# Recutting the inverse-transform stage of a two-layer spectral/MLP kernel: one tile at a time, work moved between three engines, and the DMA loads of the MLP weights moved

## The chip, the cores and the metric

The kernel runs on one core of one Trainium2 chip. The metric is the device time of one execution in microseconds (us). Engine names are those of the profile: PE is TensorE's matrix multiply, PEld its weight load, DVE is VectorE, ACT is ScalarE, POOL is GpSimd, SP is SyncE, which here only issues DMAs. A line number such as L462 is a line of the kernel that the profile belongs to, so the same statement has other numbers in other kernels.

Most executions of a kernel agree within about 0.3%, but one of the first four of the kernel before took 1096.59 us, in a state with a granted TensorE clock of 0.655 of full speed. That state is called slow. It happens to be the one that the profile caught.

## The reference, cut to what matters

```python
def _A_ref(x, w_r, w_i):                      # spectral mixer, x is (1, 2048, 576)
    X = rfft2(x.astype(float32), axes=(-2, -1))
    X = X * (w_r + 1j * w_i)
    return irfft2(X, s=(2048, 576)).astype(bfloat16)

def _B_ref(x, w1, b1, w2, b2):                # MLP, 576 -> 4608 -> 576
    y = layernorm(x)
    return gelu(y @ w1 + b1) @ w2 + b2

x = x + _A_ref(layernorm(x)); x = x + _B_ref(layernorm(x))      # layer 0
x = x + _A_ref(layernorm(x)); x = x + _B_ref(layernorm(x))      # layer 1
```

The transforms are done as matrix products. The 2048 rows are 16 tiles of 128 rows. The stage of interest is the end of `_A_ref`, once per layer: for each tile a short inverse transform along the rows (the "first product"), then the inverse transform along the 576 columns (the "second product"), which gives an even and an odd half of 288 columns. The result is x[:288] += even + odd and x[288:] += even - odd. The first four tiles are then normalised and transposed for the MLP, whose first matmul is the end of the stage.

## The kernel before

Two pools share PSUM: three big tiles of 4 KiB a partition (`big_ps`) and two small ones of half that size (`sm_ps`).

```python
def idft_v(n):                      # first product, two tiles at once
    quad, half = QUADS[n // 2], n % 2
    pu = big_ps([P, 2, 2, 2, 128])
    # ... 8 matmuls of 256 columns
    u2 = work.tile([P, 2, 2, 2, 128], BF16, tag="turn")
    nc.scalar.copy(out=u2[:], in_=pu[:])

def idft_v_rest(q):                 # last frequencies of four tiles
    # ... 16 matmuls of 128 columns into two groups of 34 partitions
    for p0 in (0, 64):
        nc.scalar.copy(out=u2r[p0 : p0 + 34], in_=pr[p0 : p0 + 34])

def idft_k(n):                      # second product and the sums, two tiles
    for i2 in range(2):
        po = big_ps([P, 2, 512])
        # ... 6 matmuls of 288 columns
        nc.vector.tensor_tensor(out=tt[:], in0=po[:, 0:1, 0:DH].to_broadcast([P, 2, DH]), in1=xr, op=ALU.add)
        marks["out", t] = nc.vector.tensor_tensor(out=xr[:, 0], in0=tt[:, 0], in1=po[:, 1, 0:DH], op=ALU.add).ins
        nc.vector.tensor_tensor(out=xr[:, 1], in0=tt[:, 1], in1=po[:, 1, 0:DH], op=ALU.subtract)

keep_busy(14)                       # matmuls on zeros while the last exchange lands
for n in range(9):
    if n < 8:
        idft_v(n)
        if n % 2 == 0: idft_v_rest(n // 2)
    if n >= 1: idft_k(n - 1)
    if n == 2: prep.stats_act()         # 8 passes on ScalarE: sum and square sum of 4 tiles
    if n == 3: prep.scale_act()
    if 4 <= n < 8: prep.norm_act(n - 4) # ScalarE
    if 5 <= n < 9: prep.turn(n - 5, "act")
    for call in loads.get(n, ()): call()
```

The first MLP weights (w1, 5.3 MB) are loaded in layer 0 through the GpSimd queue. The first two loads are released by ("h", 15), the last evacuation of the stage ahead, the others by tiles of this stage:

```python
load_w1(0, 0, ("h", 15))
load_w1(1, 0, ("h", 15))
t0, t1, t2, t3 = (("out", QUADS[q][1]) for q in range(4))
out_loads = {1: [lambda: load_w1(2, 0, t0), lambda: load_w1(3, 0, t0)], ...}   # cut
```

The stage ahead evacuates 16 tiles and sends each, right behind its evacuation, to other partitions by DMA (`exchange`, SP queue). The first product needs all 16, so it waits for the last exchange.

## Time and profile before

| | |
|---|---|
| median of 4 executions | 788.98 us (787.82 to 1096.59) |
| profiled execution | span 1094.8 us, granted clock 0.655, slow |
| MLP stages (with the forward transform of layer 1 inside the first) | 119.4 to 570 and 661.6 to 1095 us |
| inverse stages, first product to first MLP matmul | 82.9 to 118.9 and 625.8 to 661 us |

These are the lines of that profile on which the forecast rested. First the busy time by stretch. The columns are the stretch, its length, then the busy us of PE, PEld, DVE, ACT and POOL with the number of instructions, then the granted clock, the DMA engines' busy share and GB/s.

```profile
82.90:119.40 36.50, 34.41 (x245) 22.89 (x247) 24.49 (x52) 25.26 (x42) 5.89 (x12) 0.64 0.37 114
621.00:661.60 40.60, 38.48 (x258) 24.33 (x259) 24.45 (x52) 25.73 (x43) 0.95 (x4) 0.64 0.04 10
```

PE looks nearly full, but at a clock of 0.64. Scaled by that clock its 34.4 us are about 22, an estimate. DVE and ACT, whose times don't change with that clock here, have 24 to 25. So this profile can't be read as it stands.

The groups of the same stretch in layer 0 (line, engine, operation, output<-input, shapes, count, then busy us and mean ns, then idle time ahead of them):

```profile
L468 DVE TENSOR_TENSOR tt<-psb,x_sb 128x576 f32<-128x576 f32 x16 | 12.0, 753 | 17.8 <-PE psb L462 17.8
L437 ACT CAST u<-psb 128x1024 bf16<-128x1024 f32 x8 | 8.1, 1011 | 13.7 <-PE psb L432 13.7
L500 ACT ACTIVATE h_sb<-x_sb 128x576 bf16<-128x576 bf16 x8 | 5.5, 683 | 0.2
L450 ACT CAST u2r<-pss 34x512 bf16<-34x512 f32 x8 | 4.6, 579 | 0.0
```

L500 is the block of eight statistics passes. L450 shows that a copy of 34 partitions takes 579 ns for 512 columns.

### The profile page before, as it was taken

The page shows a single profiled execution, that of the slowest core. Times are in us where ns is not written, and L with a number is a line of the kernel's source. Part 1 is how long each engine was busy: PE and PEld are TensorE (multiplying, and loading weights), DVE is VectorE, ACT ScalarE, POOL GpSimd, SP SyncE. Part 2 cuts the span into 40 slices and gives each one's busy share as a digit, 9 for nine tenths or more (in the row PEclk, how much of TensorE's full clock was granted, in tenths as well). Part 3 has the DMA queues.
Part 4 walks back from the last instruction along what each step waited for, and adds up shares of the span by engine and source line. Part 5 has one row for each costly group of instructions (what it writes and reads, how often), then busy time and mean ns, then how long its engine had stood idle before and what let it go on. Part 6 is the DMA issues. An engine that isn't in the chain of part 4 may idle for free.

```text
span 1094.8 us, 12408 instructions
## 1 busy us (share of the span) xinstructions
PE 1073.5 (98%) x5159; PEld 567.6 (52%) x5195; DVE 264.2 (24%) x841; ACT 352.6 (32%) x552; POOL 46.7 (4%) x89
## 2 busy tenths in 40 slices
PE   9989999999999999999999999999999999999998
PEld 5546435653566346633665563366336633663365
DVE  6575501150033202310132674001200120010010
ACT  7647442224321442134213573420341034103400
POOL 3111000000000000000011000000000000000000
PEclk7666666666666666666666666666666666666666
DMA  7463240000000000000014202300000000000000
GB/s 227 138 186 110 90 147 1 12 7 0 1 12 12 0 1 11 7 6 0 7 39 133 83 1 87 109 6 12 6 1 6 11 6 1 6 11 6 0 12 11
DMA packets 19079, 41.58 MB, mean 38 GB/s; under 512 B 1860, under 2 KB 12944, under 8 KB 19024
## 3 DMA queue, kind: packets, MB, share of 16 engines
q0 software_dynamic: 7040, 27.88, 8.4%
q1 hardware_dynamic: 11584, 12.46, 3.8%
q8 instruction: 40, 0.66, 0.3%
q10 hardware_dynamic: 400, 0.47, 0.1%
q14 instruction: 15, 0.12, 0.0%
HBM read 28.93 MB, written 2.36 MB: 29 GB/s over the span
## 4 chain that ended last, share of the span: by engine, by line
PE 88%; issue 5%; DVE 2%; ACT 2%; DMA 2%; POOL 1%; SPq 0%; POOLq 0%; ACTq 0%; DVEq 0%
PE psb L601 38%; PE psb L560 34%; PE psb L568 5%; PE psb L462 2%; PE psb L309 2%; PE psb L432 1%; PE pss L544 1%; PE psb L376 1%; PE pss L299 1%; PE psb L402 1%; ACT h_sb L500 1%; DMA h_sb<-in_A_w_r_dram 1%; DMA b_sb<-r_sb 1%; DVE r_sb L389 1%; DVE r_sb L388 1%
## 5 line engine op out<-in xcount | busy, mean ns | idle before, releaser
L560 PE MATMUL psb<-yT,w_sb 128*128 128x512 bf16 x1120 | 377.3, 510 | 6.3 <-issue 2.0
L601 PEld LDWEIGHTS <-h_sb 128*128 128x128 bf16 x2304 | 276.3, 120 | 143.6 <-issue 3.0
L574 ACT ACTIVATE h_sb<-psb,b_sb 128x512 bf16<-128x512 f32 x288 | 176.8, 686 | 353.6 <-PE psb L568 309.9
L560 PEld LDWEIGHTS <-w_sb 128*128 128x128 bf16 x1152 | 134.0, 120 | 243.1 <-issue 241.3
L601 PE MATMUL psb<-r_sb,h_sb 128*128 128x288 bf16 x1280 | 248.5, 370 | 0.0
L601 PE MATMUL psb<-v_sb,h_sb 128*128 128x288 bf16 x1024 | 197.4, 370 | 0.0
L609 DVE TENSOR_TENSOR x_sb<-psb,xb 128x576 bf16<-128x576 f32 x32 | 24.2, 758 | 429.5 <-PE psb L601 429.5
L534 DVE TENSOR_SCALAR xn<-x_sb,mv,rs 128x576 bf16<-128x576 bf16 x24 | 9.4, 427 | 320.3 <-PE pss L544 226.6
L546 ACT COPY yT<-pss 128x640 bf16<-128x640 bf16 x32 | 22.1, 692 | 106.1 <-PE pss L544 106.1
L568 PE MATMUL psb<-yT,w1r_sb 64*128 64x512 bf16 x288 | 52.6, 493 | 0.0
L301 ACT COPY xT<-pss 96x768 bf16<-96x768 bf16 x32 | 25.2, 787 | 74.8 <-PE pss L299 74.8
L251 DVE BATCH_NORM_STATS2 stats<-x_sb 128x6 f32<-128x288 bf16 x112 | 44.6, 440 | 0.0
L314 ACT ACTIVATE z<-psb,rs 128x580 bf16<-128x580 f32 x32 | 29.3, 916 | 43.1 <-PE psb L309 42.9
L309 PE MATMUL psb<-c_fd,xT 96*128 96x290 bf16 x192 | 42.2, 372 | 0.0
L462 PE MATMUL psb<-c_gd,u 128*128 128x288 bf16 x128 | 33.7, 360 | 1.0 <-ACT u L437 0.9
L330 ACT CAST y<-psb 128x580 bf16<-128x580 f32 x24 | 15.4, 640 | 54.7 <-PE psb L327 54.7
L468 DVE TENSOR_TENSOR tt<-psb,x_sb 128x576 f32<-128x576 f32 x32 | 24.1, 753 | 32.9 <-PE psb L462 32.9
L402 PE MATMUL psb<-r_sb,h_sb 128*128 128x290 bf16 x128 | 29.3, 358 | 2.6 <-DVE r_sb L390 2.6
L568 PEld LDWEIGHTS <-w1r_sb 64*128 64x128 bf16 x288 | 10.3, 96 | 39.0 <-issue 38.3
L309 PEld LDWEIGHTS <-xT 96*128 96x128 bf16 x192 | 22.8, 119 | 12.4 <-ACT xT L301 0.4
L197 PE MATMUL pss<-zeros 128*128 128x512 bf16 x70 | 26.1, 534 | 1.6 <-DVE zeros L182 1.0
L378 ACT CAST r_sb<-psb 128x580 bf16<-128x580 f32 x32 | 20.5, 642 | 21.8 <-PE psb L376 8.4
(90 smaller groups left out, 604.5 us busy)
## 6 DMA issues: line engine op xcount, KB each, us to landing
r_sb<-in_B_w_dram POOLq DMA_DIRECT2D x4, 1440.0 KB, 7.5
w_sb<-in_B_w_dram POOLq DMA_DIRECT2D x8, 576.0 KB, 5.1
v_sb<-in_B_w_dram POOLq DMA_DIRECT2D x4, 1152.0 KB, 6.5
h_sb<-const_i POOLq DMA_DIRECT2D x8, 384.0 KB, 5.0
v_sb<-y SPq DMA_DIRECT2D x16, 145.0 KB
b_sb<-r_sb SPq DMA_DIRECT2D x16, 145.0 KB
b_sb<-y SPq DMA_DIRECT2D x16, 145.0 KB
v_sb<-r_sb SPq DMA_DIRECT2D x16, 145.0 KB
```

The source lines that it names most:

```text
L197: nc.tensor.matmul(pw[:], lhsT=zeros[:], rhs=zeros[:, 0:1].to_broadcast([P, 512]), start=True, stop=True)
L251: nc.vector.bn_stats(out=stats[:, h, :], in_=x_sb[:, t, h * DH : (h + 1) * DH])
L301: marks["turn", t] = nc.scalar.copy(out=xT[:], in_=pt[0:96]).ins
L309: nc.tensor.matmul(pz[:, o, 0:KP], lhsT=xT[:, 3 * o + ci, :], rhs=c_fd[:, 3 * o + ci, :], start=(ci == 0), stop=(ci == 2),)
L314: nc.scalar.activation(out=z[:].rearrange("p r (j o) -> p r o j", o=2), in_=pz[:, :, 0:KP].rearrange("p o (r j) -> p r o j", r=2), func=AC ...
L402: nc.tensor.matmul(ph[:, o, 0:KP], lhsT=i1[:, n % 4, pl, :], rhs=xp[:, ri, :], start=(q == 0), stop=(q == 1))
L462: nc.tensor.matmul(po[:, o, 0:DH], lhsT=lhsT, rhs=c_gd[0 : (98 if q == 2 else 128), 3 * o + q, :], start=(q == 0), stop=(q == 2),)
L560: nc.tensor.matmul(ph[:, q, :], lhsT=w1_sb[:, ci, fc * 128 : (fc + 1) * 128], rhs=yT[:, ci, :], start=(first and ci == 0), stop=(not first ...
L568: nc.tensor.matmul(acc[p][:, q, :], lhsT=w1r_sb[rows, p, :], rhs=yT[rows, 4, :], start=first, stop=not first)
L574: marks["ht", fc] = nc.scalar.activation(out=ht[:], in_=acc[p][:, q, :], func=ACT.Gelu_apprx_tanh, bias=b1_sb[:, fc : fc + 1], scale=1.0).ins
L601: nc.tensor.matmul(po[:, h, 0:DH], lhsT=hts[fc][:, i * 128 : (i + 1) * 128], rhs=w2_chunk[fc][:, h * DH : (h + 1) * DH], start=(fc == 0), ...
L609: nc.vector.tensor_tensor(out=xr, in0=po[:, :, 0:DH], in1=xb[:], op=ALU.add)
```

## The change

Its intent is to fill the holes between the three engines in this stage:

- the first product is done one tile at a time and moves to a small PSUM tile, so the big tiles serve the second product alone;
- the sums of a tile lag the next tile's first sum by one, and for five tiles (`SPLIT`) the odd half is copied out by ScalarE and subtracted by GpSimd;
- the rest frequencies become 64 columns wide, so that one copy evacuates them in place of two;
- the statistics passes are spread over seven tiles, the norms go from ScalarE to VectorE;
- all w1 loads go to the SP queue, the large ones in quarters, and start behind the first evacuation of the stage; 18 keep-busy matmuls in place of 14.

```diff
+SPLIT = (5, 7, 9, 11, 13)
...
-    def load_w1(ci, h, behind):
-        cols = slice(h * F_FF // 2, (h + 1) * F_FF // 2)
-        load(w1_sb[:, ci, cols], B_w1[ci * 128 : (ci + 1) * 128, cols], behind)
+    def load_w1(ci, h):
+        cols = slice(h * F_FF // 4, (h + 1) * F_FF // 4)
+        return nc.sync.dma_start(out=w1_sb[:, ci, cols], in_=B_w1[ci * 128 : (ci + 1) * 128, cols]).ins
...
+        def idft_v(self, n):
+            hx, t = self.hx, order[n]
+            pu = sm_ps([P, 2, 2, 128], F32)
...                                      (4 matmuls of 256 columns)
+            u2 = work.tile([P, 2, 2, 128], BF16, tag="turn")
+            marks["u2", n] = nc.scalar.copy(out=u2[:], in_=pu[:]).ins
...
+        def add(self, n):
+            if n < NT:
+                t, po = order[n], self.st["po", n]
...
+                tt_ins = nc.vector.tensor_tensor(out=tt, in0=po[:, 0:1, 0:DH].to_broadcast([P, 2, DH]), in1=xr, op=ALU.add).ins
+                if n in SPLIT:
...
+                    odd_ins = nc.scalar.copy(out=odd, in_=po[:, 1, 0:DH]).ins
+            if n > 0:
...
+                nc.vector.tensor_tensor(out=xr[:, 0], in0=tt[:, 0], in1=po[:, 1, 0:DH], op=ALU.add)
+                if n - 1 in SPLIT:
+                    nc.gpsimd.tensor_tensor(out=xr[:, 1], in0=tt[:, 1], in1=self.st.pop(("odd", n - 1)), op=ALU.subtract)
+                else:
+                    nc.vector.tensor_tensor(out=xr[:, 1], in0=tt[:, 1], in1=po[:, 1, 0:DH], op=ALU.subtract)
+
+        def run_all(self, prep, loads):
+            pieces = {n: [] for n in range(NT)}
+            for n, (i, k) in zip((1, 2, 3, 4, 5, 5, 6, 7), ((i, k) for i in range(4) for k in range(2))):
+                pieces[n].append(lambda i=i, k=k: prep.sum(i, k))
+            pieces[10].append(prep.root)
+            for i, m in enumerate((13,14,14,15)):
+                pieces[m].append(lambda i=i: prep.turn(i, "act"))
+            after_add = {9: [prep.moments], 11: [prep.scale_sums]}
+            for i, m in enumerate((11,12,12,13)):
+                after_add.setdefault(m, []).append(lambda i=i: prep.norm(i, nc.vector))
+            keep_busy(18)
+            self.idft_v(0)
+            for call in loads:
+                tc.add_manual_dep(call(), marks["u2", 0].name, SYNC, reason="pace of the loads")
+            self.idft_v_rest(0)
+            self.idft_v(1)
+            for n in range(NT):
+                self.idft_k(n)
+                self.add(n)
...                                      (what is due in after_add[n])
+                if n + 2 < NT:
+                    self.idft_v(n + 2)
...                                      (rest frequencies every fourth tile, pieces[n])
+            self.add(NT)
```

More of the change, by code (lines that the diff above doesn't have):

```diff
@@ L96, in _gd @@
         out[:, 3 * o + 1, :] = ci[main]
-        out[rest - 256, 3 * o + 2, :] = cr[rest]
-        out[64 + rest - 256, 3 * o + 2, :] = ci[rest]
+        out[rest - (KP - 64), 3 * o + 2, :] = cr[rest]
+        out[rest - (KP - 128), 3 * o + 2, :] = ci[rest]
     return out
@@ L189 @@
     nc.vector.memset(c_eps[:, 1:2], EPS * EPS)
-    for b in u2r_buf:
-        nc.vector.memset(b[:], 0.0)
     marks = {}
@@ L224, in load_f2, with load_w1r @@
         load(c_f2[:, j::4], f2_ap[:, j::4], behind)
-    def load_w1(ci, h, behind):
-        cols = slice(h * F_FF // 2, (h + 1) * F_FF // 2)
-        load(w1_sb[:, ci, cols], B_w1[ci * 128 : (ci + 1) * 128, cols], behind)
-    def load_w1r(h, behind):
+    def load_w1(ci, h):
+        cols = slice(h * F_FF // 4, (h + 1) * F_FF // 4)
+        return nc.sync.dma_start(out=w1_sb[:, ci, cols], in_=B_w1[ci * 128 : (ci + 1) * 128, cols]).ins
+    def load_w1r(h):
         rest = B_w1[512:576, :].rearrange("d (j two p) -> d two j p", two=2, p=128)
-        load(w1r_sb[64 * h : 64 * h + 64], rest[:, h], behind)
+        return nc.sync.dma_start(out=w1r_sb[64 * h : 64 * h + 64], in_=rest[:, h]).ins
     w2_parts = [at(v_sb, [P, 8, D]), at(v_sb, [P, 8, D], 8 * D), at(r_sb, [P, 10, D]), at(r_sb, [P, 10, D], 10 * D)]
@@ L418, in middle, with __init__, idft_v_rest @@
                 weigh(i)
-    cnt = [0]
-    def spectral_out(hx, prep, loads):
-        st = {}
-        def idft_v(n):
-            quad, half = QUADS[n // 2], n % 2
-            pu = big_ps([P, 2, 2, 2, 128])
-            for i2 in range(2):
-                t = quad[2 * half + i2]
-                for o in range(2):
-                    for ri in range(2):
-                        nc.tensor.matmul(
-                            pu[:, i2, o].rearrange("p a b -> p (a b)"), lhsT=hx[:, t, ri, o:256:2], rhs=c_r1[:, ri, :],
-                            start=(ri == 0), stop=(ri == 1),
-                        )
-            u2 = work.tile([P, 2, 2, 2, 128], BF16, tag="turn")
-            nc.scalar.copy(out=u2[:], in_=pu[:])
-            st["u2", n] = u2
-        def idft_v_rest(q):
+    u2r_turn = [0]
+    class SpectralOut:
+        def __init__(self, hx):
+            self.hx, self.st = hx, {}
+        def idft_v(self, n):
+            hx, t = self.hx, order[n]
+            pu = sm_ps([P, 2, 2, 128], F32)
+            for o in range(2):
+                for ri in range(2):
+                    nc.tensor.matmul(
+                        pu[:, o].rearrange("p a b -> p (a b)"), lhsT=hx[:, t, ri, o:256:2], rhs=c_r1[:, ri, :],
+                        start=(ri == 0), stop=(ri == 1),
+                    )
+            u2 = work.tile([P, 2, 2, 128], BF16, tag="turn")
+            marks["u2", n] = nc.scalar.copy(out=u2[:], in_=pu[:]).ins
+            self.st["u2", n] = u2
+        def idft_v_rest(self, q):
             pr = sm_ps([P, 4, P], F32)
@@ L445, in idft_v_rest @@
                     for ri in range(2):
-                        nc.tensor.matmul(pr[p0 : p0 + 34, i, :], lhsT=hx[:, t, ri, 256:KP], rhs=c_r1[:, ri, cs], start=(ri == 0), stop=(ri == 1))
-            u2r = u2r_buf[cnt[0] % 2]
-            cnt[0] += 1
-            for p0 in (0, 64):
-                nc.scalar.copy(out=u2r[p0 : p0 + 34], in_=pr[p0 : p0 + 34])
-            st["u2r", q] = u2r
-        def idft_k(n):
-            quad, half = QUADS[n // 2], n % 2
-            u2, u2r = st.pop(("u2", n)), st["u2r", n // 2]
-            for i2 in range(2):
-                i = 2 * half + i2
-                t = quad[i]
-                po = big_ps([P, 2, 512])
-                for o in range(2):
-                    for q, lhsT in enumerate((u2[:, i2, o, 0], u2[:, i2, o, 1], u2r[0:98, i])):
@@ L462, in idft_k @@
                         nc.tensor.matmul(
-                            po[:, o, 0:DH], lhsT=lhsT, rhs=c_gd[0 : (98 if q == 2 else 128), 3 * o + q, :],
-                            start=(q == 0), stop=(q == 2),
-                        )
-                tt = work.tile([P, 2, DH], F32, tag="f32w", bufs=2)
-                xr = x_sb[:, t, :].rearrange("p (h n) -> p h n", h=2)
-                nc.vector.tensor_tensor(out=tt[:], in0=po[:, 0:1, 0:DH].to_broadcast([P, 2, DH]), in1=xr, op=ALU.add)
-                marks["out", t] = nc.vector.tensor_tensor(out=xr[:, 0], in0=tt[:, 0], in1=po[:, 1, 0:DH], op=ALU.add).ins
@@ L470, in idft_k @@
-                nc.vector.tensor_tensor(out=xr[:, 1], in0=tt[:, 1], in1=po[:, 1, 0:DH], op=ALU.subtract)
-        keep_busy(14)
-        for n in range(9):
-            if n < 8:
-                idft_v(n)
-                if n % 2 == 0:
-                    idft_v_rest(n // 2)
-            if n >= 1:
-                idft_k(n - 1)
-            if n == 2:
-                prep.stats_act()
-            if n == 3:
-                prep.scale_act()
-            if 4 <= n < 8:
-                prep.norm_act(n - 4)
-            if 5 <= n < 9:
-                prep.turn(n - 5, "act")
-            for call in loads.get(n, ()):
-                call()
+                            pr[p0 : p0 + 64, i, :], lhsT=self.hx[:, t, ri, KP - 64 : KP], rhs=c_r1[:, ri, cs], start=(ri == 0), stop=(ri == 1)
+                        )
@@ new lines, in idft_v_rest, with idft_k @@
+            u2r = u2r_buf[u2r_turn[0] % 2]
+            u2r_turn[0] += 1
+            nc.scalar.copy(out=u2r[:], in_=pr[:])
+            self.st["u2r", q] = u2r
+        def idft_k(self, n):
+            t = order[n]
+            u2, u2r = self.st.pop(("u2", n)), self.st["u2r", n // 4]
+            po = big_ps([P, 2, 512])
+            for o in range(2):
+                for q, lhsT in enumerate((u2[:, o, 0], u2[:, o, 1], u2r[:, n % 4])):
+                    nc.tensor.matmul(po[:, o, 0:DH], lhsT=lhsT, rhs=c_gd[:, 3 * o + q, :], start=(q == 0), stop=(q == 2))
+            self.st["po", n] = po
@@ new lines, in add @@
+        def add(self, n):
+            if n < NT:
+                t, po = order[n], self.st["po", n]
+                tt = at(r_sb, [P, 2, 2 * DH], 4 * DH * (n % 3)).bitcast(F32)
+                xr = x_sb[:, t, :].rearrange("p (h n) -> p h n", h=2)
+                tt_ins = nc.vector.tensor_tensor(out=tt, in0=po[:, 0:1, 0:DH].to_broadcast([P, 2, DH]), in1=xr, op=ALU.add).ins
+                self.st["tt", n] = tt
+                if n in SPLIT:
+                    odd = at(r_sb, [P, 2 * DH], 4 * DH * 3 + 2 * DH * (n // 2 % 2)).bitcast(F32)
+                    odd_ins = nc.scalar.copy(out=odd, in_=po[:, 1, 0:DH]).ins
+                    tc.declare_no_dep(odd_ins, tt_ins, query=mybir.DependencyQuery.ANY_SYNC, reason="other bank of the product")
+                    self.st["odd", n] = odd
+            if n > 0:
+                t, po, tt = order[n - 1], self.st.pop(("po", n - 1)), self.st.pop(("tt", n - 1))
+                xr = x_sb[:, t, :].rearrange("p (h n) -> p h n", h=2)
+                nc.vector.tensor_tensor(out=xr[:, 0], in0=tt[:, 0], in1=po[:, 1, 0:DH], op=ALU.add)
[3 more added lines that the diff above has]
+                    nc.vector.tensor_tensor(out=xr[:, 1], in0=tt[:, 1], in1=po[:, 1, 0:DH], op=ALU.subtract)
@@ new lines, in run_all @@
+        def run_all(self, prep, loads):
[17 more added lines that the diff above has]
+                self.add(n)
+                for call in after_add.get(n, ()):
+                    call()
+                if n + 2 < NT:
+                    self.idft_v(n + 2)
+                if n % 4 == 1 and n + 3 < NT:
+                    self.idft_v_rest(n // 4 + 1)
+                for call in pieces[n]:
+                    call()
+            self.add(NT)
@@ L494, in __init__, with sum @@
             self.quad, self.st, self.sqrt = QUADS[q], {}, sqrt
-        def stats_act(self):
-            sums = work.tile([P, 2, 4], F32, tag="ln_sums")
-            for i, t in enumerate(self.quad):
-                for k, func in enumerate((ACT.Copy, ACT.Square)):
-                    nc.scalar.activation(out=at(h_sb, [P, D], 512 * 34), in_=x_sb[:, t, :], func=func, accum_out=sums[:, k, i : i + 1])
-            self.sums = sums
-        def scale_act(self):
-            s1, s2 = self.sums[:, 0], self.sums[:, 1]
+        def sum(self, i, k):
+            if i == 0 and k == 0:
+                self.s12 = work.tile([P, 2, 4], F32, tag="ln_sums")
+            nc.scalar.activation(
+                out=at(h_sb, [P, D], 512 * 34), in_=x_sb[:, self.quad[i], :], func=(ACT.Copy, ACT.Square)[k],
+                accum_out=self.s12[:, k, i : i + 1],
+            )
@@ L505, in scale_act, with moments @@
+        def moments(self):
             mean = work.tile([P, 4], F32, tag="ln_hv")
             var = work.tile([P, 4], F32, tag="ln_v")
-            rs = work.tile([P, 4], F32, tag="ln_rs", bufs=4)
-            shift = work.tile([P, 4], F32, tag="ln_t")
-            nc.vector.tensor_scalar(out=mean[:], in0=s1, scalar1=1.0 / D, scalar2=None, op0=ALU.mult)
-            nc.vector.tensor_mul(out=shift[:], in0=mean[:], in1=mean[:])
-            nc.vector.scalar_tensor_tensor(out=var[:], in0=s2, scalar=1.0 / D, in1=shift[:], op0=ALU.mult, op1=ALU.subtract)
@@ L512, in scale_act @@
-            nc.scalar.activation(out=var[:], in_=var[:], func=ACT.Sqrt, bias=c_eps[:, 1:2], scale=1.0 + EPS)
-            nc.vector.reciprocal(out=rs[:], in_=var[:])
-            nc.vector.scalar_tensor_tensor(out=shift[:], in0=mean[:], scalar=-1.0, in1=rs[:], op0=ALU.mult, op1=ALU.mult)
-            self.rs_shift = rs, shift
-            self.yT = work.tile([P, 5, 512], BF16, tag="yT", bufs=1, name=f"yT{uid()}")
-        def norm_act(self, i):
-            rs, shift = self.rs_shift
-            xn = work.tile([P, 640], BF16, tag="xn", bufs=3)
-            nc.scalar.activation(
-                out=xn[:, 0:D], in_=x_sb[:, self.quad[i], :], func=ACT.Identity, bias=shift[:, i : i + 1], scale=rs[:, i : i + 1]
-            )
-            nc.gpsimd.tensor_copy(out=xn[:, D:640], in_=xn[:, D - 64 : D])
-            self.st[i] = xn
+            sq = work.tile([P, 4], F32, tag="ln_t")
@@ new lines, in moments, with root @@
+            nc.vector.tensor_scalar(out=mean[:], in0=self.s12[:, 0], scalar1=1.0 / D, scalar2=None, op0=ALU.mult)
+            nc.vector.tensor_mul(out=sq[:], in0=mean[:], in1=mean[:])
+            nc.vector.scalar_tensor_tensor(out=var[:], in0=self.s12[:, 1], scalar=1.0 / D, in1=sq[:], op0=ALU.mult, op1=ALU.subtract)
+            self.mean, self.var = mean, var
+        def root(self):
+            nc.scalar.activation(out=self.var[:], in_=self.var[:], func=ACT.Sqrt, bias=c_eps[:, 1:2], scale=1.0 + EPS)
@@ L527, in stats, with scale_sums @@
+        def scale_sums(self):
+            rs = work.tile([P, 4], F32, tag="ln_rs", bufs=4)
+            nc.vector.reciprocal(out=rs[:], in_=self.var[:])
+            self.mr = [(self.mean[:, i : i + 1], rs[:, i : i + 1]) for i in range(4)]
+            self.yT = work.tile([P, 5, 512], BF16, tag="yT", bufs=1, name=f"yT{uid()}")
         def stats(self):
@@ L529, in stats, with norm @@
             self.yT = work.tile([P, 5, 512], BF16, tag="yT", bufs=1, name=f"yT{uid()}")
-        def norm(self, i):
+        def norm(self, i, engine=nc.gpsimd):
             mean, rs = self.mr[i]
@@ L536, in norm @@
             )
-            nc.gpsimd.tensor_copy(out=xn[:, D:640], in_=xn[:, D - 64 : D])
+            engine.tensor_copy(out=xn[:, D:640], in_=xn[:, D - 64 : D])
             self.st[i] = xn
@@ L666 @@
         last = li == N_LAYERS - 1
-        out_loads = {}
+        out_loads = []
         mid_loads = {}
@@ L682 @@
             nc.vector.tensor_copy(out=b1_sb[:], in_=b1p[:])
-            load_w1(0, 0, ("h", 15))
-            load_w1(1, 0, ("h", 15))
-            t0, t1, t2, t3 = (("out", QUADS[q][1]) for q in range(4))
-            out_loads = {
-                1: [lambda: load_w1(2, 0, t0), lambda: load_w1(3, 0, t0)],
-                2: [lambda: load_w1r(0, t0), lambda: load_w1r(1, t0)],
-                3: [lambda: load_w1(0, 1, t1), lambda: load_w1(1, 1, t1)],
-                5: [lambda: load_w1(2, 1, t2), lambda: load_w1(3, 1, t2)],
-            }
+            out_loads = [lambda ci=ci: load_w1(ci, 0) for ci in range(4)] + [lambda h=h: load_w1r(h) for h in range(2)]
+            out_loads += [lambda ci=ci, h=h: load_w1(ci, h) for h in range(1, 4) for ci in range(4)]
         prep = Prep(0, sqrt=True)
-        spectral_out(hx, prep, out_loads)
+        SpectralOut(hx).run_all(prep, out_loads)
         w2_loads = [lambda b, g=g: load_w2(g, b) for g in (0, 1, 2, 3)]
```

## The prediction

> **What bounds the kernel.** The profile is of a slow execution (1094.8 us, granted clock 0.655; the other three runs took 788 to 789), so PE times must be scaled. By the windows view the two MLP stages, 119 to 570 and 662 to 1095 us, take 884 us of it at 99% PE; times 0.655 that is 579 us. The change leaves them alone. It rewrites the two inverse-transform stages, 82.9 to 118.9 and 625.8 to 661 us.
>
> There PE is busy 34.4 of 36.5 us, about 22 us at full clock. The groups by shape give DVE 16 x 1.53 us start to start (three additions a tile: 0.75, 0.45, 0.45) = 24.5 us, and ACT about 26. So at full clock DVE binds, with stalls where ACT is blocked.
>
> **What the change does.**
> 1. ACT order. Before, eight statistics passes (0.81 us each) stand in one block on ACT, ahead of the next evacuation. The timeline shows ACT in them from 92.9 to 99.3 us, the fourth evacuation only then, and DVE out of tiles. Walking the dependencies by hand, with traced durations and PE at full clock, I get a 4 us hole in DVE. After, the passes are spread one or two per tile.
> 2. Granularity. Two-tile evacuations (1.01 us) become one-tile (estimate 0.58 us, from the 0.579 us of one with as many columns). DVE's first addition starts 3 us after the stage's first matmul, not 4. The big PSUM tiles hold products only, three in flight in place of two, so the MLP starts before the last two tiles are added.
> 3. Eight copies of rest columns become four: -2.3 us of ACT. Norms leave ACT (-3.5), smaller evacuations cost +1.2, five odd halves +2. Nearly even.
> 4. DVE: -5 x 0.37 us (to ACT and GpSimd), -1 from interleaving, +2 for four norms. Nearly even: the gain is fewer holes, not less work. The Trainium skill (GPSIMD Engine Reference, "Performance versus the Vector engine") puts GpSimd's two-input add at half VectorE's rate: an estimate of 0.7 to 1 us per subtraction, off the critical path.
> 5. Loads. In layer 0 two w1 loads are issued just as the last exchange leaves; it takes 6.66 us to land (chain of waits), PE idles 3 us, and the clock falls to 0.52. In layer 1, without them, PE starts 4.25 us after the same copy, against 7.0. After, all w1 loads start behind the first evacuation, on the SP queue: -3 us, once. 5.3 MB must land within 28 us; windows show bursts of 300 to 400 GB/s, so I expect no wait.
>
> **Sum.** The stage goes from 32.4 to 28.0 us, -4.4 twice, with -3 to -3.5 for the loads: -12.3 us of 789, all critical, because PE has only this stage to work on then.
>
> Predicted 776.7 us, 8 in 10 between 769 and 784; faster by over 2% 0.25, within 2% 0.72, slower 0.03.
>
> **What would show it.** A fast profile: 27 to 29 us from the first inverse matmul to the first MLP matmul; no DVE hole over 1.5 us; PE waiting 0 to 1 us for layer 0's exchange; no MLP matmul waiting for a DMA; MLP unchanged.
>
> **What would make it wrong.** w1 landing late; PE binding sooner, so the stage ends nearer 30; the four norms, queued on DVE before the last tiles, delaying the last transposes; GpSimd slower than 2.5 us per subtraction, holding a buffer; or larger stalls before than I walked, for over 2%.

## The result, and the profile after

The kernel after takes 777.25 us (median of 8 executions, 774.81 to 779.45), the kernel before 788.29. The ratio is 0.986, with a 95% interval of 0.9846 to 0.9873. Ratios here and below are the mean time of one kernel's fast runs over that of the other's of the same rounds, so they are not quite the ratio of the quoted medians. The forecast of 776.7 us holds, but its terms have to be checked one by one.

For that the kernel before was run again (a0_before, below). From the two timelines the span can be cut at five points. "Wait" is from the start of the last evacuation of the stage ahead to the first product; "stage" is from there to the first MLP matmul.

| us | before (a0_before) | after | difference |
|---|---|---|---|
| start to the last evacuation ahead, layer 0 | 69.60 | 69.70 | +0.10 |
| wait, layer 0 | 8.53 | 4.37 | -4.16 |
| stage, layer 0 | 31.86 | 26.47 | -5.39 |
| MLP, forward transform, middle | 349.06 | 348.76 | -0.30 |
| wait, layer 1 | 4.13 | 3.92 | -0.21 |
| stage, layer 1 | 29.82 | 26.48 | -3.34 |
| MLP of layer 1 to the end | 293.10 | 293.50 | +0.40 |
| span | 786.1 | 773.2 | -12.9 |

So all of it is where the change was made. The profiles differ by 12.9 us and the medians by 11, because the timed executions of the kernel after differ among themselves: they go from 774.81 us at a granted clock of 1.000 to 779.45 at 0.992, and the profiled one is of the quick kind.

The same stretch in the kernel after, layer 0, then layer 1:

```profile
74.07:102.00 27.93, 25.35 (x250) 19.08 (x252) 23.71 (x55) 22.18 (x47) 3.97 (x5) 1.00 0.65 192
453.00:481.00 28.00, 25.39 (x251) 19.00 (x252) 23.55 (x55) 22.19 (x47) 3.98 (x5) 1.00 0.01 2
```

Three engines are now busy for 22 to 25 of 28 us. The same view of the stage of layer 1 alone, before (a0_before) and then after:

```profile
463.18:493.00 29.82, 24.06 (x245) 17.84 (x246) 22.73 (x49) 24.57 (x42) 0.94 (x4) 1.00 0.01 1
453.22:479.70 26.48, 23.97 (x244) 18.42 (x245) 22.25 (x51) 20.93 (x47) 3.98 (x5) 1.00 0.00 1
```

The groups that answer to those shown of before:

```profile
L467 DVE TENSOR_TENSOR r_sb<-psb,x_sb 128x576 f32<-128x576 f32 x16 | 12.1, 754 | 8.0 <-PE psb L459 7.7
L436 ACT CAST u<-pss 128x512 bf16<-128x512 f32 x16 | 9.4, 585 | 7.2 <-PE pss L431 7.0
L450 ACT CAST u2r<-pss 128x512 bf16<-128x512 f32 x4 | 2.3, 585 | 0.0
L479 POOL TENSOR_TENSOR x_sb<-r_sb 128x288 bf16<-128x288 f32 x5 | 4.0, 793 | 39.6 <-ACT u L436 29.6 <-DVE r_sb L467 7.4 <-ACT r_sb L471 2.6
L481 DVE TENSOR_TENSOR x_sb<-r_sb,psb 128x288 bf16<-128x288 f32 x11 | 4.9, 446 | 0.0
```

The one-tile evacuation takes 585 ns (forecast 0.58 us). GpSimd's subtraction takes 793 ns where VectorE's takes 446, a factor of 1.8. The Trainium skill (GPSIMD Engine Reference, "Performance versus the Vector engine") gives 1.96 for a two-input add of 2048 fp32 elements; the trace agrees roughly, though VectorE here reads one operand from PSUM.

In layer 0 the start of the stage is where the two kernels differ most. This is the chain of waits of the kernel before (start, us, what):

```profile
70.38 7.40 DMA b_sb<-r_sb
77.78 0.35 issue
78.13 1.87 PE psb L432 x8
80.00 0.97 PE pss L446 x16
```

and of the kernel after:

```profile
69.94 3.88 PE pss L196 x17
73.82 0.25 issue
74.07 0.61 PE pss L431 x4
```

Before, the last exchange takes 7.40 us to land and its 8 matmuls of 256 columns then take 1.87 us. After, the keep-busy matmuls (L196) end last, no DMA is waited for, and 4 such matmuls take 0.61 us. The 1.87 us are a low clock, as the stretches of the kernel before show:

```profile
74.00:76.00 2.00, 0.00 (x0) 0.00 (x0) 0.00 (x0) 0.00 (x0) 0.00 (x0) 1.00 0.98 328
76.00:78.00 2.00, 0.00 (x0) 0.00 (x0) 0.00 (x0) 0.00 (x0) 0.00 (x0) 0.99 0.30 118
78.00:80.00 2.00, 1.87 (x10) 1.12 (x12) 0.00 (x0) 0.00 (x0) 0.00 (x0) 0.50 0.00 0
80.00:82.00 2.00, 2.00 (x25) 1.61 (x26) 0.00 (x0) 1.96 (x3) 0.00 (x0) 0.66 0.00 0
82.00:84.00 2.00, 2.00 (x19) 1.55 (x17) 1.02 (x2) 1.20 (x2) 0.00 (x0) 1.00 0.00 0
```

PE is idle for 5.30 us, the DMA engines are at 98% with 328 GB/s, and when PE starts again it does so at half clock, for about 3.2 us (two at 0.50, then two at 0.66 on average). The Trainium skill (TensorE: Matmul & The Clock Gate, "Part 1: The HAM clock gate") says that the array's clock falls to one half after an idle window of about 3.4 us and comes back after about 3.4 us of work; this wait agrees, with 0.50 after 5.30 us of idle time. But idle time of that length isn't needed: in b3_after_early the clock falls to 0.50 after 2.98 us, and in a0_before once more behind a gap of only 1.94 us (both below). There the measurement decides.

### The profile page after: what moved, and what is told of

Read it like the earlier page. It is cut to its first block, busy times and chain, and to the rows that moved or that the text cites. A ratio compares the mean times of both kernels' runs of the same rounds, so it can differ in the third digit from the quotient of the medians.

```text
span 773.2 us, 12486 instructions
## 1 busy us (share of the span) xinstructions
PE 739.7 (96%) x5167; PEld 463.0 (60%) x5203; DVE 261.2 (34%) x843; ACT 338.4 (44%) x562; POOL 46.8 (6%) x81
## 4 chain that ended last, share of the span: by engine, by line
PE 79%; issue 7%; DVE 6%; ACT 4%; DMA 2%; POOL 2%; SPq 0%; POOLq 0%; ACTq 0%; DVEq 0%
PE psb L617 35%; PE psb L576 33%; PE psb L584 5%; PE psb L308 2%; POOL h_sb L200 1%; ACT u L436 1%; ACT h_sb L520 1%; PE pss L196 1%; DVE r_sb L388 1%; DVE r_sb L387 1%; PE pss L560 1%; DVE r_sb L467 1%; PE psb L459 1%; DMA x_sb<-in_A_x_dram 1%; PE pss L298 1%
## 5 line engine op out<-in xcount | busy, mean ns | idle before, releaser
L576 PE MATMUL psb<-yT,w_sb 128*128 128x512 bf16 x1120 | 255.2, 379 | 4.1 <-ACT yT L562 1.6
L617 PEld LDWEIGHTS <-h_sb 128*128 128x128 bf16 x2304 | 223.8, 98 | 56.7
L576 PEld LDWEIGHTS <-w_sb 128*128 128x128 bf16 x1152 | 108.7, 98 | 145.2 <-issue 21.5
L617 PE MATMUL psb<-r_sb,h_sb 128*128 128x288 bf16 x1280 | 168.9, 286 | 0.0
L617 PE MATMUL psb<-v_sb,h_sb 128*128 128x288 bf16 x1024 | 133.6, 286 | 0.0
L584 PE MATMUL psb<-yT,w1r_sb 64*128 64x512 bf16 x288 | 39.4, 380 | 0.0
L308 PE MATMUL psb<-c_fd,xT 96*128 96x290 bf16 x192 | 30.4, 295 | 0.5 <-ACT y L329 0.4
L467 DVE TENSOR_TENSOR r_sb<-psb,x_sb 128x576 f32<-128x576 f32 x32 | 24.1, 754 | 15.7 <-PE psb L459 15.3
L459 PE MATMUL psb<-c_gd,u 128*128 128x288 bf16 x128 | 24.9, 286 | 3.3 <-DVE x_sb L481 2.1
L436 ACT CAST u<-pss 128x512 bf16<-128x512 f32 x32 | 18.7, 585 | 14.0 <-PE pss L431 13.5
```

Of the source, the lines that this page charges most:

```text
L308: nc.tensor.matmul(pz[:, o, 0:KP], lhsT=xT[:, 3 * o + ci, :], rhs=c_fd[:, 3 * o + ci, :], start=(ci == 0), stop=(ci == 2),)
L436: marks["u2", n] = nc.scalar.copy(out=u2[:], in_=pu[:]).ins
L459: nc.tensor.matmul(po[:, o, 0:DH], lhsT=lhsT, rhs=c_gd[:, 3 * o + q, :], start=(q == 0), stop=(q == 2))
L467: tt_ins = nc.vector.tensor_tensor(out=tt, in0=po[:, 0:1, 0:DH].to_broadcast([P, 2, DH]), in1=xr, op=ALU.add).ins
L576: nc.tensor.matmul(ph[:, q, :], lhsT=w1_sb[:, ci, fc * 128 : (fc + 1) * 128], rhs=yT[:, ci, :], start=(first and ci == 0), stop=(not first ...
L584: nc.tensor.matmul(acc[p][:, q, :], lhsT=w1r_sb[rows, p, :], rhs=yT[rows, 4, :], start=first, stop=not first)
```

## The experiments

Twelve kernels were run, in three jobs. Medians of different jobs are compared through the kernel before, which ran in each of them (787.85, 788.67 and 788.4 us).

### a0_before: the kernel before, unchanged

> The kernel before, unchanged, for a profile in the fast state and for the noise floor: ratio 1.000 within 0.003. If my stage walk was right, the fast profile shows 32.4 us from the first inverse matmul to the first MLP matmul in each layer (after: 26.5 in layer 0), with a hole of about 4 us in VectorE behind the statistics block, and in layer 0 about 7 us from the last middle-stage copy to the first inverse matmul (after: 4.4). Rival: the stage takes 30 us or less before and most of the 11 us came from somewhere else, the loads or the MLP.

788.44 us, ratio 1.0008 (0.9987 to 1.0029). Its stages are in the table above: 31.86 us in layer 0 and 29.82 in layer 1, against 32.4 walked by hand. What the walk had got right by its total it had partly wrong in its parts. The hole of VectorE behind the statistics block is 2.1 us in four pieces, not 4:

```profile
92.96 0.19 ACT L500 ACTIVATION_READ_ACCUMULATOR h_sb<-x_sb 128x1 f32 x1
93.17 1.01 ACT L437 CAST u<-psb 128x1024 bf16<-128x1024 f32 x1
94.24 0.42 PE L462 MATMUL psb<-c_gd,u 128*128 128x288 bf16 x2 [1.94 <-ACT u L437]
95.19 0.76 DVE L468 TENSOR_TENSOR tt<-psb,x_sb 128x576 f32<-128x576 f32 x1 [0.41 <-PE psb L462]
```

This is the timeline (start, us, engine, line, operation; in brackets the idle time just before and what ended it). The block's last pass ends at 93.15, the evacuation that stood behind it runs, PE has waited for it, and VectorE gets its next tile at 95.19. Small operations of the norm, which wait for ScalarE too, fill some of that time: from the first addition of the tile before to that of this one it is 4.6 us in place of the usual 1.5, so the block delays VectorE by 3.1 us.

Layer 0's stage is 2.04 us longer than layer 1's, and two drops of the clock make that up. The first follows the wait: VectorE's first addition starts 4.82 us into the stage, against 3.91 in layer 1, so it costs 0.9 us. The second stands behind the block. PE has the same gap there in both layers (1.94 and 1.95 us), but in layer 0 the clock is 0.63 from 94 to 98 us, in layer 1 it stays at 1.00. The same eight matmuls, layer 0 and then layer 1:

```profile
96.39 1.91 PE L432 MATMUL psb<-c_r,b_sb 128*128 128x256 bf16 x8
479.88 1.04 PE L432 MATMUL psb<-c_r,v_sb 128*128 128x256 bf16 x8
```

That costs the other 1.1 us. The traces of the runs that keep the block in the old pipeline (this one, a1_loads_only, b1_pool_later, b2_busy_bridge) have this second drop in four of their eight stages, at 0.7 to 1.3 us each, in both layers. Why it comes in one and not in the other isn't known. No stage of a2_stats_spread or of the kernel after has it.

### a1_loads_only: the kernel before with the loads of the kernel after

```diff
-            load_w1(0, 0, ("h", 15))
-            load_w1(1, 0, ("h", 15))
...
+            out_loads = [lambda ci=ci: load_w1(ci, 0) for ci in range(4)] + [lambda h=h: load_w1r(h) for h in range(2)]
+            out_loads += [lambda ci=ci, h=h: load_w1(ci, h) for h in range(1, 4) for ci in range(4)]
...                                      (load_w1 and load_w1r as in the kernel after)
+            if n == 0:
+                for call in loads:
+                    tc.add_manual_dep(call(), marks["u2", 0].name, SYNC, reason="pace of the loads")
```

> The kernel before with the change's loads alone (w1 in quarters on the SP queue, all behind the first evacuation). Theory: the last exchange lands sooner in layer 0, -2.5 to -3.5 us (785 to 786), and nothing else moves. Rival: the loads are worth nothing by themselves because PE waits for the keep-busy matmuls anyway: 788.

781.75 us, ratio 0.9917 (0.9898 to 0.9937): -6.1 us against the 787.85 of the same job, twice what was expected. The profile cuts it in two. The wait in layer 0 falls from 8.53 to 4.25 us, and the stage that follows from 31.86 to 29.82, the same as in layer 1 (29.83). The last exchange now lands in 3.09 us, PE waits 1.02 us for it, and the clock stays up:

```profile
70.66 3.09 DMA b_sb<-r_sb
73.75 0.38 issue
74.12 1.05 PE psb L432 x8
```

So with the loads moved 4.3 us of wait and 2.0 us of low clock are gone: 6.1 of the 11.0 us by time, 6.3 of 12.9 by profile, about half of the whole change. Of the 2.0 us only 0.9 follow from the wait. The other 1.1 are the drop behind the block, which this profile doesn't have; whether the loads have a part in that is open. The wait is as short with the 14 keep-busy matmuls of this run as with the 18 of the kernel after (4.25 and 4.37 us), so the four more gained nothing.

### b1_pool_later: only the first two loads moved, on their old queue

```diff
-            load_w1(0, 0, ("h", 15))
-            load_w1(1, 0, ("h", 15))
...
+                0: [lambda: load_w1(0, 0, ("u2", 0)), lambda: load_w1(1, 0, ("u2", 0))],
                 1: [lambda: load_w1(2, 0, t0), lambda: load_w1(3, 0, t0)],
```

> The kernel before with only its first two w1 loads moved: same queue (GpSimd), same halves, but behind the first evacuation of the stage in place of the last copy of the middle stage. Theory (when they are issued is what costs: they share the DMA engines with the last exchange): the same as all loads moved, 781.5 to 782.5 us. Rival (the SP queue or the quarters matter): it stays near 788, or lands between.

783.64 us (781.40 to 785.61), ratio 0.9933 (0.9918 to 0.9949), against 0.9917 for a1_loads_only: the intervals overlap. Its two executions at a granted clock of 1.000 took 781.40 and 781.74 us, the same as a1_loads_only, whose four ran at 0.999 to 1.000. The four others, at 0.991 to 0.996, took 782.81 to 785.61. In the profiled one (784.47 us, at 0.991) the wait is 4.23 us, as it should be, and the 2.6 us that its span is longer than that of a1_loads_only lie elsewhere: 0.7 us ahead of the wait (the clock is 0.79 from 8 to 16 us), 1.3 and 0.7 us in the two stages (31.07 and 30.51 us), where the clock drops behind the block, in layer 1 too, where no w1 is loaded. So when the loads are issued is what counts, not the queue or the piece size. The Trainium skill (DMA: Bandwidth & Descriptors, "Queues, rings and completion order") says that each DMA engine takes turns between the queues it has work for. That fits: loads issued within a microsecond of the exchange, on another queue, would share its engines. The runs show the delay (7.40 against 3.09 us), not the turns.

### b2_busy_bridge: the wait kept, the idle time filled

```diff
-        keep_busy(14)
+        keep_busy(38 if loads else 14)
```

> The kernel before with 38 keep-busy matmuls in place of 14 ahead of layer 0's inverse stage, so that TensorE is never idle while the last exchange lands; the wait itself stays. Theory (of the 6.3 us that the loads are worth, 4.2 are the wait and 2.0 the lower clock after the idle time): 785.5 to 786.5 us, stage of layer 0 29.8 us in place of 31.9, first inverse matmul still about 8.5 us after the last copy. Rival (the longer stage of layer 0 comes from w1 traffic in the stage, not from the clock): 788.

788.46 us, ratio 1.0003 (0.999 to 1.0016): a miss in the total, a hit against the rival. The stage of layer 0 takes 29.83 us at a clock of 1.00, as without the loads, although the same w1 traffic runs in it. So the 2.0 us are low clock and not traffic. It is one profiled execution, and both drops of a0_before are absent from it; that only 0.9 us of the two follow from the wait is read from a0_before. But the 38 matmuls took too long. The clock happened to be low when they started:

```profile
69.00:72.00 3.00, 2.67 (x8) 1.13 (x9) 0.38 (x2) 0.64 (x1) 1.06 (x2) 0.51 0.36 98
72.00:74.00 2.00, 2.00 (x9) 0.84 (x8) 0.00 (x0) 0.00 (x0) 0.00 (x0) 0.89 0.87 296
78.00:80.00 2.00, 2.00 (x14) 1.14 (x12) 0.00 (x0) 0.00 (x0) 0.00 (x0) 1.00 0.00 0
```

The wait became 9.91 us in place of 8.53, and that, with 0.7 us more in the stage of layer 1 (30.52 us, with a drop of the clock behind the block), ate the gain. Filling a wait with work of fixed length costs as soon as the work outlasts the wait. Taking the wait away is better.

### b3_after_early: the kernel after with two loads early again

```diff
+            for ci in range(2):
+                load(w1_sb[:, ci, 0 : F_FF // 2], B_w1[ci * 128 : (ci + 1) * 128, 0 : F_FF // 2], ("h", 15))
...                                      (the rest as in the kernel after)
```

> The kernel after with two half loads of w1 issued again on the GpSimd queue behind the last middle-stage copy. Theory: 5 to 6.5 us come back (782 to 784), as wait for the exchange and low clock. Rival (the finer stage absorbs the wait): within 2 us of 777.

781.63 us, ratio 0.9917 (0.9905 to 0.993), against 0.986 for the kernel after: 0.57% or 4.5 us come back, a little under the expected range. In the profile, that of the slowest of its executions (784.18 us), the wait of layer 0 is 8.31 us (+3.9) and its stage 28.02 (+1.5): PE is idle for 2.98 us, and from 2 to 4 us into the stage the clock is 0.50. Layer 1's stage, which the edit doesn't touch, is 26.46.

### a2_stats_spread: the kernel before with the statistics spread

```diff
-            if n == 2:
-                prep.stats_act()
-            if n == 3:
+            if 2 <= n < 6:
+                prep.stats_act(n - 2)      # two passes
+            if n == 5:
                 prep.scale_act()
...                                      (norms at n = 6, 6, 7, 7; transposes at 7, 7, 8, 8)
```

> The kernel before with the eight statistics passes spread two per step, and the scale, norms and transposes that depend on them packed into the last three steps; all else as before. Theory (the ScalarE block makes the VectorE hole): -2 to -4 us per layer, 781 to 784, part of the gain given back at the stage's end where norms now crowd. Rival (finer evacuations and a third product slot make the gain): within 1 us of 788.

786.65 us, ratio 0.9984 (0.9966 to 1.0001): hardly anything. The stage of layer 1 goes from 29.82 to 29.34 us. The holes are really gone: VectorE's first to last addition takes 26.25 us in place of 28.10, and its idle time in between is 1.54 in place of 3.19. But the last addition now ends 0.81 us after the first MLP matmul in place of 2.18. The norms, transposes and their evacuations, which had been hidden in the middle of the stage, stand at its end. 1.85 us were gained on VectorE, and 1.4 given back at the end. The view of that stage, to be held against 29.82 us of the kernel before:

```profile
462.29:491.63 29.34, 24.41 (x244) 17.86 (x245) 23.90 (x52) 24.14 (x42) 0.94 (x4) 1.00 0.00 1
```

In layer 0 the stage goes from 31.86 to 30.26 us: the same 0.5, and the 1.1 of the second clock drop, which isn't there without the block. What remains over layer 1, 0.92 us, is the drop after the wait. My theory for the gain of the stage, that the block makes the hole and the hole makes the time, falls with this run as the whole cause: the block, taken away in this way, is worth 0.5 us a layer, and a clock drop where there was one. The run doesn't test the block alone, as the same edit packs the norms into the last steps.

### a3_stats_block: the kernel after with the statistics in one block

```diff
-            for n, (i, k) in zip((1, 2, 3, 4, 5, 5, 6, 7), (
+            for n, (i, k) in zip((4, 4, 4, 4, 4, 4, 4, 4), (
```

> The kernel after with all eight statistics passes in one block on ScalarE at tile 4. Theory (the block is what costs): 2 to 4 us per layer come back, 781 to 785. Rival (the finer pipeline hides a block): within 1 us of 777.

788.91 us, ratio 1.0017 (0.9998 to 1.0037): with the block the whole change is worth nothing, all of its 11 us come back. The stage takes 33.02 us in layer 1, 6.5 more than without the block and 3.2 more than in the kernel before. The timeline of layer 1:

```profile
475.16 0.59 ACT L436 CAST u<-pss 128x512 bf16<-128x512 f32 x1
475.29 0.46 DVE L477 TENSOR_TENSOR x_sb<-r_sb,psb 128x288 bf16<-128x288 f32 x1 [3.72 <-ACT r_sb L471]
475.80 1.01 PE L431 MATMUL pss<-c_r,v_sb 128*128 128x256 bf16 x4 [5.02 <-ACT u L436]
478.29 0.76 DVE L467 TENSOR_TENSOR r_sb<-psb,x_sb 128x576 f32<-128x576 f32 x1 [2.54 <-PE psb L459]
```

The small PSUM tiles hold the first product of one tile each, so PE can run only two tiles ahead. It stands still for 5.02 us until ScalarE evacuates, VectorE waits 3.72 us for an odd half that stands behind the block as well, and PE resumes at a lower clock: the four matmuls take 1.01 us in place of 0.60. The windows view gives 0.50 for that time, and this low clock is part of the 6.5 us:

```profile
474.00:478.00 4.00, 2.20 (x10) 1.43 (x10) 0.46 (x1) 2.79 (x8) 0.79 (x1) 0.50 0.00 0
```

### c1_big_pool: the kernel after with the first product in a big PSUM tile

```diff
-            pu = sm_ps([P, 2, 2, 128], F32)
+            pu = big_ps([P, 2, 2, 2, 128])[:, 0]
```

> The kernel after, but the one-tile inverse product takes a big PSUM tile again, as before, so that only two of the three big tiles serve the second product at a time. Theory (the third product slot lets TensorE run ahead): 1 to 3 us per layer come back, 779 to 783. Rival (the finer evacuation alone makes the earlier start and the fewer holes): within 1 us of 777.

787.97 us, ratio 1.0003 (0.9984 to 1.0022): one line takes the whole gain away, and with it more than the stage had given, since the moved loads are still in (wait 4.22 us in layer 0). The stage takes 32.76 us in layer 1, 6.3 more than the kernel after. The timeline shows a closed loop:

```profile
466.57 0.41 PE L459 MATMUL psb<-c_gd,u 128*128 128x288 bf16 x2 [0.73 <-ACT u L436]
467.30 0.60 PE L431 MATMUL psb<-c_r,v_sb 128*128 128x256 bf16 x4
467.50 0.76 DVE L467 TENSOR_TENSOR r_sb<-psb,x_sb 128x576 f32<-128x576 f32 x1 [0.58 <-PE psb L459]
467.94 0.59 ACT L436 CAST u<-psb 128x512 bf16<-128x512 f32 x1 [0.75 <-PE psb L431]
468.58 0.41 PE L459 MATMUL psb<-c_gd,u 128*128 128x288 bf16 x2 [0.67 <-ACT u L436]
```

From one second product to the next it is 2.01 us: second product, first product of a later tile, its evacuation, and only then the next second product. Sixteen of these are 32 us. VectorE stands idle 0.4 to 1.0 us ten times, 6.95 us in all with the smaller gaps. Which tile of the pool each product is given was not traced, so that the second product takes the PSUM tile just evacuated is my reading of the wait, not a measurement.

### b4_no_split: no work for GpSimd

```diff
-SPLIT = (5, 7, 9, 11, 13)
+SPLIT = ()
```

> The kernel after with no tile split: VectorE does all odd halves, ScalarE and GpSimd none. Theory (VectorE and ScalarE are both near full, VectorE binds the second half of the stage): 0.4 to 1.5 us per layer come back, 778 to 780. Rival (ScalarE is what binds, 2 us of its work per layer go away): 774 to 776, faster than after.

778.92 us, ratio 0.9879 (0.9866 to 0.9892), against 0.986 (0.9846 to 0.9873) for the kernel after; the intervals overlap, so the times alone don't part them. By profile the stage is 27.10 and 27.03 us in place of 26.47 and 26.48, so the split is worth 0.6 us a layer, within what was expected of VectorE binding.

### c2_copies_gpsimd, c3_turns_earlier, c4_more_splits: further along the same way

In the kernel after, the chain of waits of the stage's second half runs along VectorE and ends so:

```profile
98.17 0.37 DVE x_sb L481
98.54 0.04 issue
98.59 0.90 PE psb L459 x6
99.48 0.29 PE pss L560 x5
99.78 0.02 issue
99.80 0.70 ACT yT L562
```

VectorE releases a PSUM tile, the last second product runs, and then the last transpose and its evacuation stand between it and the MLP. Three edits, each on top of the one before:

```diff
-    ... prep.norm(i, nc.vector)              # c2: the 64-column copies of the norms
+    ... prep.norm(i)                         #     on GpSimd, as elsewhere in the kernel
-            for i, m in enumerate((13,14,14,15)):   # c3: transposes
+            for i, m in enumerate((12,13,14,14)):
-            for i, m in enumerate((11,12,12,13)):   # c3: norms
+            for i, m in enumerate((11,12,12,12)):
-SPLIT = (5, 7, 9, 11, 13)                    # c4: and three odd buffers in turn
+SPLIT = (7, 9, 10, 11, 12, 13)
```

> The kernel after with the four small copies of a norm (64 columns) on GpSimd, as the MLP and the kernel before have them, not on VectorE. Theory (VectorE binds the second half of the stage): 0.5 to 1 us per layer less, 775 to 776. Rival (GpSimd's latency or its subtractions delay the transposes): 777 or more.

> As c2_copies_gpsimd, with the fourth norm one tile earlier and the four transposes at tiles 12, 13, 14, 14, so that none stands between the last product and the MLP. Theory (the stage ends with: last product waits for VectorE, then transpose, evacuation, MLP): about 1 us per layer less than c2_copies_gpsimd, 773 to 774.5. Rival (the same waits move forward: TensorE waits for the norms at tile 12): no gain.

> As c3_turns_earlier, with the split tiles 7, 9, 10, 11, 12, 13 in place of 5, 7, 9, 11, 13 and three odd buffers: one more VectorE pass off in the VectorE-bound half, none on ScalarE in the ScalarE-bound half. Theory: 0.3 to 0.8 us per layer less than c3_turns_earlier, 772 to 773.5. Rival (GpSimd, at 0.8 us each, now falls behind and holds PSUM or odd buffers): no gain or a loss.

| | median us | ratio to before (95%) | stage, layer 0 / layer 1 |
|---|---|---|---|
| after | 777.25 | 0.986 (0.9846 to 0.9873) | 26.47 / 26.48 |
| c2_copies_gpsimd | 775.83 | 0.9837 (0.9818 to 0.9857) | 25.83 / 25.84 |
| c3_turns_earlier | 773.88 | 0.9817 (0.9797 to 0.9837) | 25.34 / 25.26 |
| c4_more_splits | 773.58 | 0.9809 (0.9792 to 0.9827) | 24.87 / 24.84 |

Each step shortens the stage, by 0.64, 0.5 to 0.6 and 0.4 to 0.5 us a layer. The first is as expected; the second is half of what was expected; the MLP's first matmul then waits for VectorE to release its PSUM tile (0.23 us in the timeline of layer 0), and the rest of the shortfall wasn't traced. The third is as expected in the stage, but in time it can't be told from the step before; its profile has 5.09 us of wait in layer 1 in place of 3.91, with the clock at 0.56 in its first 3 us. The intervals of the kernel after and of c2_copies_gpsimd overlap too, so this step rests on its stage times. The results of all twelve kernels are correct. c4_more_splits beats both kernels: its interval lies below that of the kernel after, 0.5% further down, though it ran in another job.

## Why the prediction was right

The total, 777.25 us against 776.7, is well within the range, and the class "within 2%" was given 0.72. Point by point:

- **What binds.** That PE doesn't fill the stage at full clock was right, but its scaled 22 us were low: it is busy 24.1 us of layer 1's 29.8 before (a0_before), more than DVE's 22.7. "DVE binds" was wrong for the kernel before: the chain of waits of that stage runs for 11.7 us over PE, 9.6 over ACT and 8.2 over DVE. The stage before was forecast at 32.4 us and took 31.86 and 29.82.
- **Step 5, loads.** The mechanism was right, the term mis-sized. "-3 us, once" (-3 to -3.5 in the sum) was the wait alone, read from the slow profile as 7.0 less 4.25. It measured 4.2 to 4.3 (a1_loads_only, b1_pool_later), and the low clock right after it another 0.9 (a0_before), which the forecast saw ("the clock falls to 0.52") but gave at most half a microsecond. Together 5.2 us by profile.
- **The sum, "-4.4 twice".** Mis-sized: the stage alone gained 3.34 us (layer 1). The 5.39 of layer 0 hold 2.0 of low clock, 0.9 after the wait and 1.1 behind the statistics block. So the profiles differ by 5.1 (4.2 and 0.9) + 1.1 + 2 x 3.34 = 12.9 us, where the forecast had 3.5 + 8.8 = 12.3. The loads and the clock gave more than forecast and the stage less; that the two errors cancelled was luck.
- **Step 1, the statistics block.** The hole is real, but VectorE is idle for 2.1 us and late by 3.1, not 4, and removing it is worth 0.5 us a layer at full clock (a2_stats_spread). What the forecast didn't have is the clock drop behind the hole, 0.7 to 1.3 us in some stages and none in others. This step failed as a cause of the gain. The runs show in its place that no part does it alone. The block costs 6.5 us in the new pipeline, its low clock included (a3_stats_block), the shared PSUM pool 6.3 (c1_big_pool), while the whole stage gained 3.3: the parts are conditions of each other and their worths don't add up.
- **Step 2, granularity.** VectorE's first addition starts 2.66 us after the first matmul, 3.90 before: as forecast. The third product slot was counted as a help at the stage's end. It is a condition for the finer tiles to pay at all. That the MLP starts ahead of the last additions was true before as well (2.18 us ahead in layer 1, 1.72 after), so nothing was gained there.
- **Steps 3 and 4, work on ACT and DVE.** Nearly even was forecast. From first product to MLP in layer 1, ACT went from 24.57 to 20.93 us busy and DVE from 22.73 to 22.25. ACT fell by more than my own items (-2.6) sum to. GpSimd took 0.79 us a subtraction, in the forecast 0.7 to 1. Without the split 1.2 us come back, in both layers together.
- **What would show it.** No VectorE hole over 0.41 us in the kernel after; no wait for the exchange in layer 0; no MLP matmul waiting for a DMA (w1, 5.31 MB, landed before the stage's end); MLP unchanged within 0.4 us. All as forecast but the stage, which ended sooner: 26.5 us against 27 to 29.

What stays open: how VectorE's stage gain divides between one-tile evacuations, the lag of the sums and the narrower rest frequencies, which were only run together; and why the clock drops behind equal gaps of PE in one execution or layer and not in another, by which the granted clock of otherwise equal executions varies between 0.99 and 1.00.

## What to carry to other kernels

Look at what else is on the DMA engines when a short transfer stands on the critical path: two prefetches issued within a microsecond of it more than doubled its landing time (7.40 us against 3.09), and TensorE then ran at half clock for about 3 us. When you compare stages, compare their clocks too: here 1.1 us of a stage came from a drop that the layer beside it didn't have. When a pipeline is cut finer, give each product its own PSUM pool and spread every side job, since in this kernel a single block on the evacuating engine or a shared pool took back the whole gain. And read a slow-state profile only after scaling: the engine that is 94% busy there need not be the one that binds.

## What the Trainium skill lacked or had wrong

- TensorE: Matmul & The Clock Gate, Part 1, names granted clocks of one half, full and 13/16 (and one quarter, in a caveat on its records). A whole execution at 0.655 (1096.59 us against 788), with nothing in the kernel to cause it, is in none of the pages that I read.
- TensorE: Matmul & The Clock Gate gives the price of an idle window for matmul streams. For a stage that three engines share, the price measured here is 0.9 us for one idle gap of 5.30 us (first addition 4.82 us into the stage, against 3.91).
- TensorE: Matmul & The Clock Gate, Part 1, puts the fall to half clock after an idle window of about 3.4 us. Here it also fell to 0.50 after 2.98 us (b3_after_early), and behind gaps of 1.94 us at most in four of eight stages, at 0.7 to 1.3 us each. The page tells of shorter idle times too, but with no size and no price.
- DMA: Bandwidth & Descriptors describes the turns between queues, but gives no price for a short transfer behind bulk loads: here 145 KB took 7.40 us to land beside two loads of 576 KB issued just after it, against 3.09 without them.
- None of the pages that I read gives a price for sharing a PSUM pool between a producer's and a consumer's product: here 6.3 us in a stage of 26.5 (c1_big_pool).
